# An exact integer addition of a weight conversion goes from VectorE to GpSimd, with another hand-written order of the opening

## The chip, the cores and the metric

One core of a Trainium2 chip runs the whole program. The metric is the device time of one execution in microseconds (us). "PE" is TensorE, "DVE" VectorE, "ACT" ScalarE, "POOL" GpSimd, and "SP" the engine whose queue issues most DMAs.

## The reference

Eight batches of an attention with two sparse masks (a local one for the first four heads, a strided one for the other four), then a feed-forward block on the 4608 tokens. The weights come as 64-bit floats.

```
scores = scale * np.matmul(q, k.transpose(0, 1, 3, 2))      # 8 x 8 heads, 576 x 576, D = 64
mask_local = (rel >= 0) & (rel < 32)
mask_strided = (rel >= 0) & (pos[None, :] % 32 == pos[:, None] % 32)
attn = softmax(where(mask, scores, -1e9));  x = attn @ v      # (4608, 512)
h = np.maximum(np.maximum(x @ w1, x @ w2), x @ w3)            # 512 -> 768
out = h @ w_out                                               # 768 -> 512
```

## The kernel before

Tokens are worked in nine chunks of 512. Attention goes in 32 units of two heads: units 0 to 3 are batch 0, 4 to 7 batch 1, and within a batch the first two are strided, the last two local. Every float32 matrix product is made of three float32r products (high times high, high times low part, low times high).

Each of the 24 weight tiles (128 x 512 values; 0 to 17 for w1, w2, w3, then 18 to 23 for w_out) lands as 64-bit words, and the kernel builds the float32 value out of the bits before it splits it into a high and a low part. Up to the end of the first chunk (chunk 0) all engines follow one order written out by hand, the string `OPENING`, in steps of a letter and a number. Each engine takes its own instructions in just this order. The letters:

- A: ACT takes the magnitude of the high words (L144) and scales the low words (L145); POOL clamps the magnitude (L146). The result lies in a `work` tile, of which there are three in turn.
- B: three DVE instructions. L158 shifts the bits into a scratch that lies in the upper halves of two banks of the PSUM tile `o_ps`; L161 joins them with the sign bits; L164 adds the rounding as an integer. The trace shows L164 as a custom DVE operation on 1024 elements of 16 bits.
- C: ACT copies the high part (L172), POOL subtracts to get the low part (L173). The `work` tile is free after that.
- S, X, E, N: scores on PE, less maximum on DVE, exponential on ACT, sums, probabilities and a transpose on DVE, for one unit. V: values on PE into `o_ps`. H and L: ACT (L417) and DVE (L421) copy `o_ps` out as high and low parts; `o_ps` is a single tile, so the next V waits for L.
- F: 12 matmuls of the first product for chunk 0 (L436) into one of two `f_ps` tiles; F of number n uses weight tile n. M: the maximum, by ACT (L447) or DVE (L449), and after every third the split by ACT (L452) and POOL (L453). O and Q: second product (18 matmuls, L462), copy and store. U: a rearranging copy on ACT.

In matmuls of PE, S of a unit below 8 has 132 in a strided unit (4 that write the mask, L257, and 128, L288) and 76 (4 and 72) in a local one; V has 128 (L400) in a strided unit of batches 0 and 1 and 84 (L359) in a local one. All loads stand in SP's queue in one order: the operands of units 0 to 3 with weight tiles between them, then weights and units 4 and 5; the loads of later units are issued at S and V. After the opening, chunks 1 to 8 run in a loop that the diff doesn't touch.

Before, PE's part of the order up to its first F is S0 S1 S2 V0 S3 V1 V2 S4 V3 F0.

Of the kernel before, what the change touches and what calls it, by code (L numbers as in the profile page):

```python
# [9 lines left out]
I32 = mybir.dt.int32  # L10
U32 = mybir.dt.uint32
AF = mybir.ActivationFunctionType
ALU = mybir.AluOpType
AX = mybir.AxisListType

B, H, S, D = 8, 8, 576, 64
# [28 lines left out]


OPENING = """
A0 S0 X0 E0 N0 S1 X1 B0 E1 S2 A1 N1 C0 X2 V0 A2 B1 B2 H0 C1 S3 A3 L0 X3 V1 E2 E3 N2 C2 H1 L1 V2 N3 A4 S4
H2 A5 L2 B3 C3 X4 E4 B4 C4 V3 H3 N4 L3 F0 A6 B5 A7 F1 C5 B6 M0 C6 M1 A8 S5 B7 X5 C7 A9 B8 E5 F2 F3 C8 M2
N5 V4 A10 A11 M3 F4 B9 C9 B10 F5 C10 H4 M4 A12 S6 M5 X6 A13 F6 B11 B12 F7 M6 C11 L4 F8 C12 B13 E6 M7 A14  # L50
C13 V5 A15 A16 F9 M8 B14 C14 B15 A17 B16 M9 C15 B17 A18 C16 A19 F10 M10 F11 C17 B18 F12 C18 M11 H5 M12
N6 F13 A20 F14 L5 A21 B19 V6 C19 A22 M13 F15 B20 C20 M14 F16 M15 A23 F17 B21 M16 B22 C21 C22 S7 M17 B23
X7 C23 H6 O0 E7 L6 N7 U8 O1 Q0 O2 V7 S8 Q1 H7 L7 O3 Q2 Q3
"""


# [1 line left out]
def fused_kernel(ctx, tc, qT, kT, qk_loc, qk_str, v_loc, v_str, m_loc, m_str, w1, w2, w3, w_out, out):  # L58
    nc = tc.nc
# [20 lines left out]
    pin = tc.keep_in_program_order  # L80
# [17 lines left out]
    for sign in (1, -1):  # L98
        pin(nc.gpsimd.affine_select(
            out=unit, in_=unit, pattern=[[-sign, P]], base=0, channel_multiplier=sign, compare_op=ALU.is_ge, fill=0.0  # L100
# [21 lines left out]
    raws, begun, weight = [], [], {}  # L122
# [14 lines left out]
    def convert_begin():  # L137


        raw, i, j = raws.pop(0)  # L140
        words = raw.rearrange("p (n two) -> p n two", two=2)
        low, high = words[:, :, 0], words[:, :, 1]
        mag = wk.tile([P, 512], F32, name="work")
        pin(nc.scalar.activation(out=mag, in_=high.bitcast(F32), func=AF.Abs))  # L144
        pin(nc.scalar.activation(out=low, in_=low.bitcast(U32), func=AF.Copy, scale=2.0**-29))  # L145
        pin(nc.gpsimd.tensor_scalar(out=mag, in0=mag, scalar1=W_MOST, scalar2=W_LEAST, op0=ALU.min, op1=ALU.max))  # L146
        begun.append((low, high, mag, i, j))

    converted = []

    def convert_bits():

        low, high, mag, i, j = begun.pop(0)
        banks = len(weight) + len(converted)
        psum = o[:, banks % 2 * 2 : banks % 2 * 2 + 2, 256:].bitcast(I32)
        bits = mag.bitcast(I32)
        halves = lambda x: x.rearrange("p (a f) -> p a f", a=2)
        pin(nc.vector.tensor_scalar(  # L158
            out=psum, in0=halves(bits), scalar1=3, scalar2=0x3FFFFFF8, op0=ALU.logical_shift_left, op1=ALU.bitwise_and
        ))  # L160
        pin(nc.vector.scalar_tensor_tensor(  # L161
            out=halves(bits), in0=halves(high), scalar=-0x40000000, in1=psum, op0=ALU.bitwise_and, op1=ALU.bitwise_or
        ))
        pin(nc.vector.tensor_tensor(out=bits, in0=bits, in1=low, op=ALU.add))  # L164
        converted.append((mag, i, j))

    def convert_end():

        mag, i, j = converted.pop(0)
        parts = wt.tile([P, 2, 512], F32R, name=f"w{i}_{j}")  # L170
        hi, lo = parts[:, 0, :], parts[:, 1, :]
        pin(nc.scalar.copy(out=hi, in_=mag))  # L172
        pin(nc.gpsimd.tensor_tensor(out=lo, in0=mag, in1=hi.bitcast(F32), op=ALU.subtract))  # L173
        weight[i, j] = [x if i is None else x.rearrange("p (c f) -> p c f", c=NKC) for x in (hi, lo)]
# [251 lines left out]
    def ff_in(c, j, i):  # L426
        if not ps_f:
            early_ps.close()
            ps_f.append(ctx.enter_context(tc.tile_pool(name="ps_f", bufs=2, space=bass.MemoryType.PSUM)))
        f_ps = ps_f[0].tile([P, 512], F32, name="f_ps")  # L430
        hi, lo = x_chunk(c)
        wh, wl = weight[i, j]

        for kc in (2, 3, 0, 1):
            for n, (w, x) in enumerate(((wh, hi), (wh, lo), (wl, hi))):
                pin(nc.tensor.matmul(  # L436
                    f_ps, w[:, kc, :], x[:, kc, :], start=(kc == 2 and n == 0), stop=(kc == 1 and n == 2)
                ))
        hs[c, j, i] = f_ps

    def ff_max(c, j, i):
        f_ps = hs.pop((c, j, i))
        if i == 0:
            hs[c, j] = hm.tile([P, CH], F32, name="h_max")
        a = hs[c, j]
        if i == 0:
            pin(nc.scalar.copy(out=a, in_=f_ps))  # L447
        else:
            pin(nc.vector.tensor_tensor(out=a, in0=f_ps, in1=a, op=ALU.max))  # L449
        if i == 2:  # L450
            hh, hl = hs[c, j] = hp.tile([P, CH], F32R, name="hh"), hp.tile([P, CH], F32R, name="hl")
            pin(nc.scalar.copy(out=hh, in_=a))  # L452
            pin(nc.gpsimd.tensor_tensor(out=hl, in0=a, in1=hh.bitcast(F32), op=ALU.subtract))  # L453
# [24 lines left out]
    for n in (2, 3):  # L478
# [9 lines left out]
    steps = {  # L488
        "U": paired_queries, "S": scores, "X": less_maximum, "E": exponentials, "N": lambda n: (probabilities(n), transposed(n)),
        "V": values, "H": leading, "L": rest,  # L490
        "A": lambda n: convert_begin(), "B": lambda n: convert_bits(), "C": lambda n: convert_end(),
        "F": lambda n: ff_in(0, n // 3, n % 3), "M": lambda n: ff_max(0, n // 3, n % 3),
        "O": lambda n: ff_out(0, n), "Q": lambda n: ff_store(0, n),
    }
    for step in OPENING.split():
        what, n = step[0], int(step[1:])
# [8 lines left out]
    for c in range(1, NCHUNK):  # L505
# [4 lines left out]
        for i in range(3 * NJ + CH // P):  # L510
            if i in BURSTS and c < B - 1:
                n = 4 * (c + 1) + BURSTS.index(i)
# [98 lines left out]
```

## Time and profile before

| | |
|---|---|
| median of 3 runs | 716.47 us (713.24 to 718.65) |
| the profiled execution | 712.11 us |
| its span, first to last instruction | 710.4 us |
| PE busy | 680.8 us (96%) |
| DVE, ACT, POOL busy | 311.7, 185.3, 122.6 us |
| first F matmul | 46.44 us after the start |

The profiled execution has its own time. The page gives busy time by engine; the windows give it by stretch; the timeline shows each engine's instructions in order, with the idle time before them in brackets and what ended it. "issue" there is a wait that no semaphore in the profile explains.

### The profile page before, as it was taken

To read this page: it belongs to the slowest core of one execution; us is meant where nothing else is said; L and a number is where in the kernel's file an instruction comes from. 1 tells how busy PE (TensorE), PEld (TensorE's weight loads), DVE (VectorE), ACT (ScalarE), POOL (GpSimd) and SP (SyncE) were. 2 spreads that over 40 slices of the span, in tenths; PEclk is the share of its full clock that TensorE was granted. 3 is DMA by queue.
4 is the path that set the end of the run, shared out by engine and by line. 5 is a ranking of instruction groups with operands and counts; after the bars stand their busy time and mean duration, and the time that the engine had idled before them with its cause. 6 is when DMAs were issued, how large, how long until landed. Compare 5 with 4: busy or idle time off the path is not lost.

```text
span 710.4 us, 17277 instructions
## 1 busy us (share of the span) xinstructions
PE 680.8 (96%) x7680; PEld 559.6 (79%) x7680; DVE 311.7 (44%) x527; ACT 185.3 (26%) x394; POOL 122.6 (17%) x129
## 2 busy tenths in 40 slices
PE   5469899999999999999999999999999999999997
PEld 4358677888888888888888888888888888888886
DVE  5778996455504551444344443544155201101110
ACT  1546563312222222213122222222222111111111
POOL 4336573001101110111001100110001101100110
PEclk9869999999999999999999999999999999999999
DMA  8998101222311222112321231223120010010001
GB/s 238 269 303 305 52 31 64 96 72 73 102 48 55 64 85 94 55 56 65 109 70 54 65 102 51 81 66 93 42 64 2 16 45 1 0 43 17 1 1 59
DMA packets 35803, 55.26 MB, mean 78 GB/s; under 512 B 5200, under 2 KB 18512, under 8 KB 35728
## 3 DMA queue, kind: packets, MB, share of 16 engines
q1 hardware_dynamic: 30016, 44.19, 21.3%
q10 hardware_dynamic: 5712, 9.96, 3.8%
q8 instruction: 60, 0.98, 0.6%
q14 instruction: 15, 0.12, 0.1%
HBM read 44.70 MB, written 9.44 MB: 76 GB/s over the span
## 4 chain that ended last, share of the span: by engine, by line
PE 88%; DVE 4%; DMA 2%; issue 2%; POOL 1%; ACT 1%; SPq 1%; DVEq 0%; POOLq 0%; ACTq 0%
PE f_ps L436 59%; PE f_ps L462 20%; PE o_ps L359 2%; PE s_ps L288 2%; PE o_ps L389 2%; PE s_ps L266 2%; DMA w<-in_w 2%; DVE work L164 1%; DVE work L161 1%; DVE o_ps L158 1%; SPq L228 1%; POOL wNone L173 1%; PE o_ps L400 0%; DMA v_t<-in_v_loc 0%; DVE xl L421 0%
## 5 line engine op out<-in xcount | busy, mean ns | idle before, releaser
L436 PE MATMUL f_ps<-xh,w 128*128 128x512 f32 x1296 | 409.2, 392 | 2.8 <-ACT h_max L447 1.8
L436 PEld LDWEIGHTS f_ps<-xh,w 128*128 128x128 f32 x1296 | 243.9, 188 | 56.5 <-ACT h_max L447 2.3
L436 PE MATMUL f_ps<-xl,w 128*128 128x512 f32 x648 | 252.9, 390 | 0.0
L449 DVE TENSOR_TENSOR h_max<-f_ps,h_max 128x512 f32<-128x512 f32 x108 | 74.4, 689 | 286.1 <-PE f_ps L436 285.9
L453 POOL TENSOR_TENSOR hl<-h_max,hh 128x512 fp32r<-128x512 f32 x54 | 69.4, 1286 | 516.5 <-ACT hh L452 516.5
L436 PEld LDWEIGHTS f_ps<-xl,w 128*128 128x128 f32 x648 | 122.0, 188 | 24.5
L462 PE MATMUL f_ps<-wNone,hh 128*128 128x512 f32 x432 | 134.2, 392 | 0.2 <-POOL wNone L173 0.2
L462 PEld LDWEIGHTS f_ps<-wNone,hh 128*128 128x128 f32 x432 | 80.5, 188 | 17.4 <-POOL wNone L173 0.7
L452 ACT CAST hh<-h_max 128x512 fp32r<-128x512 f32 x54 | 33.4, 619 | 197.8 <-DVE h_max L449 197.8
L462 PE MATMUL f_ps<-wNone,hl 128*128 128x512 f32 x216 | 84.1, 389 | 0.0
L421 DVE TENSOR_TENSOR xl<-o_ps,xh 128x320 fp32r<-128x320 f32 (+11 forms) x96 | 28.3, 350 | 55.5 <-ACT xh L417 44.7
L447 ACT COPY h_max<-f_ps 128x512 f32<-128x512 f32 x54 | 31.7, 587 | 62.8 <-POOL hl L453 32.0
L467 ACT COPY work<-f_ps 128x512 f32<-128x512 f32 x36 | 21.2, 588 | 101.5 <-PE f_ps L462 101.5
L462 PEld LDWEIGHTS f_ps<-wNone,hl 128*128 128x128 f32 x216 | 40.5, 188 | 8.5
L316 ACT ACTIVATE s_ps<-s_ps 128x640 f32<-128x640 f32 (+2 forms) x32 | 20.2, 633 | 88.3 <-DVE s_ps L312 87.8
L417 ACT CAST xh<-o_ps 128x320 fp32r<-128x320 f32 (+11 forms) x96 | 24.3, 328 | 32.2 <-PE o_ps L389 18.8
L333 DVE STREAM_TRANSPOSE pt<-s_ps 128x640 f32<-128x640 f32 (+2 forms) x32 | 31.3, 979 | 0.7
L288 PE MATMUL s_ps<-qk_t 64*32 64x64 f32 (+1 forms) x1664 | 22.6, 227 | 7.1 <-issue 5.1
L311 DVE TENSOR_REDUCE mx<-s_ps 128x10 f32<-128x640 f32 (+2 forms) x32 | 24.1, 752 | 10.0 <-PE s_ps L288 9.2
L288 PEld LDWEIGHTS s_ps<-qk_t 64*32 64x32 f32 x1664 | 19.3, 117 | 11.4 <-issue 8.6
L173 POOL TENSOR_TENSOR w<-work,w 128x512 fp32r<-128x512 f32 x18 | 23.4, 1301 | 25.6 <-ACT w L172 25.6
L359 PEld LDWEIGHTS o_ps<-pt,v_t 32*64 32x64 f32 x1344 | 17.6, 141 | 10.6 <-issue 6.2
(52 smaller groups left out, 362.3 us busy)
## 6 DMA issues: line engine op xcount, KB each, us to landing
out<-work ACTq DMA_DIRECT2D x36, 256.0 KB
w<-in_w SPq DMA_DIRECT2D x17, 512.0 KB
qk_t<-in_qT SPq DMA_DIRECT2D x28, 288.0 KB
qk_t<-in_kT SPq DMA_DIRECT2D x28, 288.0 KB
v_t<-in_v_str SPq DMA_DIRECT2D x48, 128.0 KB
v_t<-in_v_loc SPq DMA_DIRECT2D x48, 96.0 KB
wNone<-in_w_out SPq DMA_DIRECT2D x6, 512.0 KB
v_t<-in_v_str SPq DMA_DIRECT2D x16, 72.0 KB
```

The source lines that it names most:

```text
L173: pin(nc.gpsimd.tensor_tensor(out=lo, in0=mag, in1=hi.bitcast(F32), op=ALU.subtract))
L288: pin(nc.tensor.matmul(s_ps[32 * j : 32 * (j + 1), h, k1 : k1 + w], t[hs, q0 : q0 + 32], t[hs, k0 : k0 + w], start=not first, stop=not fir ...
L333: pin(nc.vector.transpose(pt[:, :, : nm * at], s_ps[:, :, : nm * at]))
L359: pin(nc.tensor.matmul(o[h * D : (h + 1) * D, j, 32 * max(m, 0) : 32 * max(m, 0) + width], v[js, h, m + 1, :], pt[js, h, m * TK + 32 : m * ...
L417: pin(nc.scalar.copy(out=hi, in_=src))
L421: pin(nc.vector.tensor_tensor(out=lo, in0=src, in1=hi.bitcast(F32), op=ALU.subtract))
L436: pin(nc.tensor.matmul(f_ps, w[:, kc, :], x[:, kc, :], start=(kc == 2 and n == 0), stop=(kc == 1 and n == 2)))
L447: pin(nc.scalar.copy(out=a, in_=f_ps))
L449: pin(nc.vector.tensor_tensor(out=a, in0=f_ps, in1=a, op=ALU.max))
L452: pin(nc.scalar.copy(out=hh, in_=a))
L453: pin(nc.gpsimd.tensor_tensor(out=hl, in0=a, in1=hh.bitcast(F32), op=ALU.subtract))
L462: pin(nc.tensor.matmul(f_ps, h[:, ts], w, start=(j == 0 and n == 0), stop=(j == NJ - 1 and n == 2)))
```

## The change

The third instruction of B, the integer addition, becomes a step of its own, D, as a plain integer `tensor_tensor` on GpSimd. C follows D. The scratch's place alternates as before. The order of the opening is another one; on PE it now goes S0 S1 V0 S2 S3 V1 V2 S4 V3 F0, and S7 stands ahead of V6. The order of the loads ahead of the opening is the same.

```diff
--- before.py
+++ after.py
@@ -45,12 +45,13 @@
 
 
 OPENING = """
-A0 S0 X0 E0 N0 S1 X1 B0 E1 S2 A1 N1 C0 X2 V0 A2 B1 B2 H0 C1 S3 A3 L0 X3 V1 E2 E3 N2 C2 H1 L1 V2 N3 A4 S4
-H2 A5 L2 B3 C3 X4 E4 B4 C4 V3 H3 N4 L3 F0 A6 B5 A7 F1 C5 B6 M0 C6 M1 A8 S5 B7 X5 C7 A9 B8 E5 F2 F3 C8 M2
-N5 V4 A10 A11 M3 F4 B9 C9 B10 F5 C10 H4 M4 A12 S6 M5 X6 A13 F6 B11 B12 F7 M6 C11 L4 F8 C12 B13 E6 M7 A14
-C13 V5 A15 A16 F9 M8 B14 C14 B15 A17 B16 M9 C15 B17 A18 C16 A19 F10 M10 F11 C17 B18 F12 C18 M11 H5 M12
-N6 F13 A20 F14 L5 A21 B19 V6 C19 A22 M13 F15 B20 C20 M14 F16 M15 A23 F17 B21 M16 B22 C21 C22 S7 M17 B23
-X7 C23 H6 O0 E7 L6 N7 U8 O1 Q0 O2 V7 S8 Q1 H7 L7 O3 Q2 Q3
+A0 S0 X0 B0 E0 D0 C0 S1 N0 X1 E1 N1 V0 S2 H0 L0 A1 A2 B1 X2 E2 S3 D1 B2 V1 D2 A3 C1 C2 H1 N2 X3 A4 B3 D3
+B4 L1 E3 D4 A5 C3 N3 V2 C4 H2 B5 S4 A6 B6 L2 D5 X4 D6 V3 C5 A7 C6 H3 L3 A8 A9 F0 B7 D7 B8 M0 D8 C7 F1 B9
+D9 F2 A10 C8 M1 E4 C9 M2 B10 F3 A11 N4 A12 D10 M3 F4 B11 M4 D11 B12 S5 F5 V4 C10 C11 D12 A13 M5 C12 X5
+B13 F6 A14 M6 F7 D13 E5 A15 B14 M7 F8 B15 D14 N5 C13 D15 A16 F9 C14 C15 H4 M8 A17 F10 M9 A18 S6 B16 F11
+M10 D16 B17 D17 C16 X6 C17 B18 A19 E6 D18 M11 L4 B19 A20 F12 F13 V5 C18 N6 D19 M12 B20 M13 A21 F14 D20
+B21 C19 H5 D21 C20 F15 A22 C21 A23 M14 L5 B22 D22 B23 D23 M15 C22 F16 M16 S7 C23 F17 X7 E7 M17 V6 O0 O1
+H6 L6 N7 U8 Q0 V7 S8 H7 O2 Q1 O3 Q2 Q3 L7
 """
 
 
@@ -151,7 +152,7 @@
     def convert_bits():
 
         low, high, mag, i, j = begun.pop(0)
-        banks = len(weight) + len(converted)
+        banks = len(weight) + len(converted) + len(added)
         psum = o[:, banks % 2 * 2 : banks % 2 * 2 + 2, 256:].bitcast(I32)
         bits = mag.bitcast(I32)
         halves = lambda x: x.rearrange("p (a f) -> p a f", a=2)
@@ -161,7 +162,14 @@
         pin(nc.vector.scalar_tensor_tensor(
             out=halves(bits), in0=halves(high), scalar=-0x40000000, in1=psum, op0=ALU.bitwise_and, op1=ALU.bitwise_or
         ))
-        pin(nc.vector.tensor_tensor(out=bits, in0=bits, in1=low, op=ALU.add))
+        added.append((low, mag, i, j))
+
+    added = []
+
+    def convert_add():
+        low, mag, i, j = added.pop(0)
+        bits = mag.bitcast(I32)
+        pin(nc.gpsimd.tensor_tensor(out=bits, in0=bits, in1=low, op=ALU.add))
         converted.append((mag, i, j))
 
     def convert_end():
@@ -488,7 +496,8 @@
     steps = {
         "U": paired_queries, "S": scores, "X": less_maximum, "E": exponentials, "N": lambda n: (probabilities(n), transposed(n)),
         "V": values, "H": leading, "L": rest,
-        "A": lambda n: convert_begin(), "B": lambda n: convert_bits(), "C": lambda n: convert_end(),
+        "A": lambda n: convert_begin(), "B": lambda n: convert_bits(), "D": lambda n: convert_add(),
+        "C": lambda n: convert_end(),
         "F": lambda n: ff_in(0, n // 3, n % 3), "M": lambda n: ff_max(0, n // 3, n % 3),
         "O": lambda n: ff_out(0, n), "Q": lambda n: ff_store(0, n),
     }
```

## Rows read from the trace of the kernel before

**Rows 1.** The page: busy time by engine, and the granted clock in 40 slices.
```profile
PE 680.8 (96%) x7680; PEld 559.6 (79%) x7680; DVE 311.7 (44%) x527; ACT 185.3 (26%) x394; POOL 122.6 (17%) x129
PEclk9869999999999999999999999999999999999999
```

**Rows 2.** Windows: length; busy us of PE, PEld, DVE, ACT, POOL; clock, DMA share, GB/s.
```profile
0.00:46.44 46.44, 23.94 (x972) 19.13 (x972) 30.98 (x58) 15.96 (x31) 16.00 (x38) 0.81 0.96 271
46.44:116.00 69.56, 66.28 (x862) 52.42 (x858) 64.00 (x98) 42.76 (x82) 44.95 (x44) 0.98 0.43 134
116.00:710.40 594.40, 590.59 (x5852) 488.01 (x5852) 216.68 (x372) 126.59 (x283) 61.64 (x48) 1.00 0.18 56
```

**Rows 3.** Timeline of PE, 12 to 47 us: start, us, what, [idle before].
```profile
12.39 0.67 PE L288 MATMUL s_ps<-qk_t 64*32 64x18 f32 x42 [2.21 <-issue]
12.98 2.50 PE L257 MATMUL s_ps<-mloc,unit 128*128 128x320 f32 x4
15.41 1.36 PE L288 MATMUL s_ps<-qk_t 64*32 64x64 f32 x72
...
19.98 1.92 PE L400 MATMUL o_ps<-pt,v_t 18*64 18x18 f32 x120 [2.86 <-issue]
...
24.26 1.24 PE L288 MATMUL s_ps<-qk_t 64*32 64x64 f32 x72
27.89 0.79 PE L400 MATMUL o_ps<-pt,v_t 18*64 18x18 f32 x59 [2.38 <-DVE xl L421]
30.80 1.26 PE L400 MATMUL o_ps<-pt,v_t 18*64 18x18 f32 x69 [2.13 <-issue]
33.72 1.26 PE L359 MATMUL o_ps<-pt,v_t 32*64 32x64 f32 x59 [1.66 <-DVE xl L421]
36.10 0.67 PE L359 MATMUL o_ps<-pt,v_t 32*64 32x64 f32 x25 [1.12 <-issue]
...
41.97 0.44 PE L288 MATMUL s_ps<-qk_t 64*32 64x18 f32 x30 [2.85 <-issue]
44.86 1.66 PE L359 MATMUL o_ps<-pt,v_t 32*64 32x64 f32 x84 [2.44 <-DVE work L161]
46.44 0.80 PE L436 MATMUL f_ps<-xh,w 128*128 128x512 f32 x1
```

**Rows 4.** DMA queues, 17 to 18 and 39 to 40 us: packets, MB, share.
```profile
q8 instruction: 1, 0.02, 9.5%
...
q8 instruction: 1, 0.02, 7.2%
```

**Rows 5.** Timeline of PE after F0: its two longest idle times.
```profile
87.62 0.50 PE L436 MATMUL f_ps<-xh,w 128*128 128x512 f32 x1 [1.85 <-ACT h_max L447]
...
91.41 0.50 PE L436 MATMUL f_ps<-xh,w 128*128 128x512 f32 x1 [0.77 <-DVE h_max L449]
```

**Rows 6.** Groups by line and shape, 0 to 150 us: busy us, mean ns.
```profile
L173 POOL TENSOR_TENSOR w<-work,w 128x512 fp32r<-128x512 f32 x18 | 23.4, 1301 | 25.6 <-ACT w L172 25.6
...
L158 DVE TENSOR_SCALAR o_ps<-work 128x512 int32<-128x512 int32 x24 | 16.5, 687 | 3.4 <-PE o_ps L400 2.2 <-POOL work L146 0.5 <-PE o_ps L359 0.3
L146 POOL TENSOR_SCALAR work<-work 128x512 f32<-128x512 f32 x24 | 15.7, 659 | 22.1 <-ACT work L144 22.0
L164 DVE CUSTOM_DVE_ANT_0 work<-w,work 128x1024 uint16<-128x1024 uint16 x18 | 15.6, 869 | 1.7
...
L161 DVE SCALAR_TENSOR_TENSOR work<-w,o_ps 128x512 int32<-128x512 int32 x18 | 12.4, 687 | 0.7
...
L453 POOL TENSOR_TENSOR hl<-h_max,hh 128x512 fp32r<-128x512 f32 x7 | 9.1, 1299 | 25.9 <-ACT hh L452 25.9
...
L164 DVE CUSTOM_DVE_ANT_0 work<-wNone,work 128x1024 uint16<-128x1024 uint16 x6 | 6.5, 1084 | 0.6
```

**Rows 7.** Lines L164 and L173: durations, shortest, median, longest ns.
```profile
L164 DVE CUSTOM_DVE_ANT_0 work<-wNone,work x6: 693/782/1805, 92.9 to 112.0; 128x1024 uint16<-128x1024 uint16 x6
...
L173 POOL TENSOR_TENSOR w<-work,w x18: 1265/1290/1523, 21.3 to 94.7; 128x512 fp32r<-128x512 f32 x18
```

## The prediction

> **What bounds the kernel now.** I read the page first: PE is busy for 96% of the span, and the granted clock is full from the fourth slice on [rows 1]. Then three windows, cut at the first F (46.44 us) and at the end of O0 (116 us) [rows 2]. After 116 us PE is idle for 3.8 us in 594: nothing that this change touches can shorten that. Between 46.44 and 116 PE is idle for 3.28 us of 69.56, with DVE busy for 64.0 and POOL for 44.95. Ahead of 46.44 it is idle for 22.5 us. So all that can be won or lost lies in two sums, 22.5 us ahead of F0 and 3.3 us behind it; PE's work itself doesn't change.
>
> Ahead of F0 the timeline of PE shows what the idle time waits for [rows 3]. Five of the waits, 2.21, 2.86, 2.13, 1.12 and 2.85 us, 11.2 in all, are called "issue" and fall in the middle of a step, where no semaphore is waited for. Counting matmuls by the steps' sizes (132, 132, 76, 128, 76, 128, 84, 132 for S0 S1 S2 V0 S3 V1 V2 S4), the rows restart at matmul 222 (42 of S1 are left), 348 (120 of V0 left), 603 (69 of V1), 731 (25 of V2) and 858 (30 of S4). The distances are multiples of about 127; the one place that is missing, about 476, lies in S3. With its weight load a matmul is two instructions, so this is a grid of some 254 instructions. The DMA view shows packets of an instruction queue, one of 0.02 MB, in 17 to 18 us and in 39 to 40 us, shortly ahead of the restarts at 19.98 and 41.97 [rows 4]. So PE waits there for its own program, which comes by DMA while the DMA engines are 0.96 busy [rows 2]. The times fit a window of two blocks, the next being asked for when one is used up: matmul 476 was passed at about 24.3 and 603 restarted at 30.80, 6.5 us later; 603 was reached at 28.68 and 731 came at 36.10, 7.4 later; 731 was reached at 34.98 and 858 came at 41.97, 7.0 later [rows 3].
>
> The Trainium skill ("Runtime: NRT & Kernel Launch", section "Instruction fetch mechanics") has just this window of two 16 KiB blocks of 256 instructions, but says that crossing a block is mostly hidden. By that rule the 11.2 us would have another cause, and the new order could not lose by them; this is the first rival below. The trace disagrees while the loads fill the DMA engines.
>
> **The change part by part.** *DVE loses the addition*: 18 at 869 ns and 6 at 1084 ns [rows 6], 15.6 + 6.5 = 22.1 us. Some 19 of them lie behind F0, where DVE was 92% busy and where PE's two long waits, 1.85 and 0.77 us, are for the emptying of `f_ps` by ACT and DVE [rows 5], held up in the queues of conversions. With DVE down from 64.0 to about 45 us of 69.6 these waits go; I keep 0.4 of the 3.28 us of idle time. What is late next there is POOL.
>
> *POOL gains 24 integer additions.* None is in the trace. The nearest row is its subtraction L173, also two inputs of 512 values, at 1301 ns [rows 6], hardly ever longer than 1290 (longest 1523) [rows 7]. The lower end is the clamp with one input, 659 ns [rows 6]. The upper end is two subtractions, 2.6 us, if POOL had to go by halves of 16 bits as the record of the DVE operation does (1024 elements [rows 6]). I take 1.29, the row with the same number of inputs: 24 x 1.29 = 31 us more, beside PE's matmuls. Behind F0 POOL then has 17 tiles (seven are converted ahead of F0 in the new order) of 0.66 + 1.29 + 1.29 and six h splits of 1.30 [rows 6], 55.1 + 7.8 = 62.9 us. PE has 66.3 us of work up to the end of O0 [rows 2], whose last group, 0.7 us, is the first to need POOL's last results. So POOL fits, with 2.7 us to spare. It is nearly full, and I expect PE to wait little for it: only the w_out tiles come just in time, since tiles 7 to 17 are needed at 2.8 us each plus attention and POOL delivers one in 3.7 us with a lead of seven.
>
> The Trainium skill ("GPSIMD Engine Reference", section "Key points") speaks against the move: elementwise work is about twice as fast on VectorE. By that rule, at 1.29 for 0.69 us and with every addition on the path, the change would cost 24 x 0.6 = 14 us. The rows agree on the durations: the shortest L164 took 693 ns. But beside POOL's work it took up to 1805 ns, while POOL's subtraction hardly stretched [rows 7], and the addition lies beside matmuls; so I take nothing of the 14 us.
>
> *The order ahead of F0.* V0 now goes ahead of S2. V0 can start when S1 ends (about 13.05), runs 84 matmuls to number 348 and stands until 19.98 as before, since that block was asked for when S1 passed 222, which hasn't moved. Before, this wait was filled by S2, 2.50 + 1.36 us, with only 8 of V0 [rows 3]; now only V0's 84, 1.3 us, stand ahead of it and S2 comes after. Matmul 476 is passed at 19.98 + 0.7 (44 of V0) + 3.8 (S2) + 2.5 (the mask matmuls of S3) = 27.0 instead of 24.3. The next block follows 6.5 us later, at 33.5 (30.80 before); V1 ends at 34.8.
>
> Then B3 and B4 now stand ahead of L1 on DVE; before they came behind V2. They write their scratch into `o_ps`, so they wait for V1 and H1, as L158 is seen to wait for L400 [rows 6]; V2 waits for L1. From V1's end to V2 it was 1.66 us [rows 3]; with two B of 0.687 + 0.687 [rows 6] it is 4.4: V2 starts at 39.3 and reaches 731 at 40.5 (34.98 before). The block behind comes 7.0 later, 47.5; S4's last 30 matmuls 0.44, V3 1.66, and F0 starts at 49.6. Before, V3 waited another 2.44 us for the L161 of a B [rows 3]; now S4 is later than DVE and that wait is gone. So F0 is 49.6 - 46.44 = 3.1 us later: two block waits carry +5.5, less 2.44.
>
> *What moves at no cost*: D0, C0 and the early conversions lie on POOL and ACT, which were busy for 16 of 46 us ahead of F0 [rows 2]; if POOL were late there, C6 would still not be needed before F6. S7 ahead of V6 changes the order of two loads in SP's queue, for units of the next chunk. O2 behind V7 and S8 is work that PE has in either order. At F0 PE starts at the same reduced clock as before, after the same idle time [rows 1].
>
> *The sum*: +3.1 ahead of F0, -2.9 behind it: +0.2 us on the profiled execution's 712.11, 712.3. That execution was 4.4 us below the median of the runs, 716.47; against the median I forecast 716.7.
>
> **The rivals.**
> 1. *The blocks don't hold PE* (the fetch is not tied to the position in the program, or the later requests find shorter queues). For it: the one at about 476 cost nothing. Against it: five restarts on the grid. If only the first came as early as before, F0 would be at 32.06 + 1.66 + 2.75 + 1.26 + 7.0 + 0.44 + 1.66 = 46.8, +0.4 and -2.5 in all; with neither, V2 ends at 38.2, S4 takes 2.8 (its own time before, without the wait) and V3 1.66, so 42.7, -3.7 and -6.6 in all. DVE's B5, B6 and L2 stand ahead of V3 and keep it from the lower end: I take -4.5, 712.0.
> 2. *POOL becomes the bound, slower.* It decides from the point where 17 additions use up the 2.7 us to spare, 1.29 + 0.16 = 1.45 us each. At 1.9 us it is 17 x 0.45 = 7.7 us behind F0, less the waits already gone: +0.2 + 7.7 = about 724; at 2.6 us 19.6, 736. For it: the stride of 8 bytes in the low words and an integer type that no POOL row shows. Against: the flat 1.29 of two-input rows.
> 3. *The blocks take longer.* The one asked for at 222 (10.18) came at 19.98, 9.8 us later [rows 3]. With that for both, F0 is 3.3 + 2.8 = 6.1 us later still: 722.8.
> 4. *The addition is lowered to something else than one POOL instruction*: then POOL's row isn't there and DVE keeps its 22 us; the order alone would give 3.1 us and up to the old 3.3 behind F0, +3.1 or about 719.6.
>
> **How the numbers follow.** Forecast 0.52, rival 1 0.2, rival 2 0.12, rival 3 0.13, rival 4 0.03. About 1%, 7.2 us, is what a measurement of this kernel can tell from no change: the three runs lie 5.4 us apart. Faster by more needs more than rival 1's lower end: 0.06 with the scatter. Slower by more: rival 2 from 1.9 us, and the upper end of rival 3 with the scatter, 0.13. The rest, 0.81, is within. The range goes from 711 (rival 1, with a us of scatter) to 724 (rivals 2 at 1.9 us and 3); left out are rival 2's dearer prices.
>
> **What the profile after would show.** The addition as a POOL row of 24 near 1.29 us; DVE near 289.6 us, POOL near 153.6. PE's "issue" waits at matmuls 222, 348, 603 and 858 again; no restart before 19.98 in V0, with some 5 us of idle time there; F0 near 49.6; behind F0 less than 1 us of idle time on PE. Wrong would be: an F0 ahead of 46.5 (the count of blocks or the wait of B3 for H1 is wrong), a POOL addition over 1.45 us, or PE waiting for POOL in O0.

## The result

The changed kernel takes 707.33 us (706.89 to 707.39, four runs) against 715.92 us (713.24 to 718.65, four runs) of the kernel before: the ratio is 0.9879, with an interval of 0.984 to 0.9917. It is faster by 1.2%, and its time lies below the predicted range. The profiled execution took 707.39 us, that of before 712.11.

The page of the changed kernel: busy time by engine, the granted clock in 40 slices, and the shares of the chain that ended last.

```profile
PE 680.0 (96%) x7680; PEld 560.5 (79%) x7680; DVE 290.5 (41%) x503; ACT 185.6 (26%) x394; POOL 151.3 (21%) x153
PEclk9769999999999999999999999999999999999999
PE 94%; DVE 2%; DMA 1%; issue 1%; SPq 1%; ACT 0%; POOL 0%; POOLq 0%; DVEq 0%
```

DVE has 21.2 us less than in [rows 1], POOL 28.7 more, PE the same work. Windows of the changed kernel, cut at its first F and at 116 us, with the columns of [rows 2]:

```profile
0.00:42.00 42.00, 21.73 (x973) 17.87 (x973) 29.21 (x54) 19.23 (x36) 27.54 (x48) 0.81 0.90 269
42.00:116.00 74.00, 72.43 (x914) 58.45 (x909) 47.65 (x83) 41.48 (x81) 61.98 (x58) 0.95 0.45 147
116.00:705.70 589.70, 585.89 (x5827) 484.18 (x5808) 213.64 (x366) 124.91 (x277) 61.77 (x48) 1.00 0.18 56
```

F0 starts at 42.00 instead of 46.44 us. Behind it PE is idle for 1.57 of 74.00 us instead of 3.28 of 69.56, with DVE at 64% of that stretch (92% before) and POOL at 84% (65% before). The timeline of PE in the changed kernel shows both; its lines answer to [rows 3] (S is L265 and L296 now, V L408 and L367, F L444):

```profile
10.99 0.66 PE L296 MATMUL s_ps<-qk_t 64*32 64x18 f32 x42 [0.90 <-issue]
13.05 1.47 PE L408 MATMUL o_ps<-pt,v_t 18*64 18x18 f32 x85 [1.39 <-DVE pt L341]
15.28 0.88 PE L408 MATMUL o_ps<-pt,v_t 18*64 18x18 f32 x43 [0.77 <-issue]
16.09 2.50 PE L265 MATMUL s_ps<-mloc,unit 128*128 128x320 f32 x4
...
25.30 1.75 PE L408 MATMUL o_ps<-pt,v_t 18*64 18x18 f32 x128 [3.44 <-DVE work L162]
33.40 1.65 PE L367 MATMUL o_ps<-pt,v_t 32*64 32x64 f32 x84 [6.35 <-DVE xl L429]
36.36 1.32 PE L265 MATMUL s_ps<-mstr,unit 128*128 128x144 f32 x4 [1.31 <-DVE pt L341]
...
40.05 0.44 PE L296 MATMUL s_ps<-qk_t 64*32 64x18 f32 x29 [1.26 <-issue]
40.42 1.65 PE L367 MATMUL o_ps<-pt,v_t 32*64 32x64 f32 x84
42.00 0.80 PE L444 MATMUL f_ps<-xh,w 128*128 128x512 f32 x1
...
64.93 0.82 PE L408 MATMUL o_ps<-pt,v_t 18*64 18x18 f32 x63 [1.57 <-issue]
```

The waits named "issue" still fall at the same counts, 222 (42 of S1 left), 349 (43 of V0 left), 859 (29 of S4 left) and, behind F0, 1241 (63 of V4 left). But ahead of F0 they are 0.90, 0.77 and 1.26 us, 2.9 in all where before had 11.2, and V3's wait of 2.44 us is gone. Behind F0 there is one wait only, in V4; no F waits for ACT or DVE as in [rows 5]. A wait named "issue" at such a count is called a block wait below. The addition itself, by line and shape, and then shortest, median and longest:

```profile
L172 POOL TENSOR_TENSOR work<-work,w 128x512 int32<-128x512 int32 x18 | 23.4, 1300 | 5.3 <-DVE work L162 3.6 <-POOL work L172 0.8 <-POOL w L181 0.4
L172 POOL TENSOR_TENSOR work<-work,wNone 128x512 int32<-128x512 int32 x6 | 7.8, 1311 | 0.5 <-DVE work L162 0.5
L172 POOL TENSOR_TENSOR work<-work,w x18: 1278/1300/1327, 11.1 to 83.5; 128x512 int32<-128x512 int32 x18
```

It is one POOL instruction of 1.30 us, as long as the subtraction [rows 7] and flatter.

One quantity orders all that follows: the start of chunk 1, which is the first L436 or L444 behind O3 on PE's timeline. In ten profiled executions of the two kernels the time is that start plus 581.1 to 581.2 us, so the whole difference lies ahead of it: 131.04 us before, 126.18 after. Each run below is told by its median time and the ratio to the kernel before in the same session, then by F0 and the stretch from F0 to chunk 1 in its profiled execution.

### The profile page after: what moved, and what is told of

Read it like the earlier page. It is cut to its first block, busy times and chain, and to the rows that moved or that the text cites. A ratio compares the mean times of both kernels' runs of the same rounds, so it can differ in the third digit from the quotient of the medians.

```text
span 705.7 us, 17268 instructions
## 1 busy us (share of the span) xinstructions
PE 680.0 (96%) x7680; PEld 560.5 (79%) x7680; DVE 290.5 (41%) x503; ACT 185.6 (26%) x394; POOL 151.3 (21%) x153
## 4 chain that ended last, share of the span: by engine, by line
PE 94%; DVE 2%; DMA 1%; issue 1%; SPq 1%; ACT 0%; POOL 0%; POOLq 0%; DVEq 0%
PE f_ps L444 64%; PE f_ps L470 21%; PE o_ps L367 2%; PE s_ps L296 2%; PE o_ps L397 2%; PE s_ps L274 2%; DMA w<-in_w 1%; SPq L236 1%; PE s_ps L265 1%; PE o_ps L408 0%; DVE o_ps L159 0%; DVE work L162 0%; DVE pt L341 0%; DVE s_ps L334 0%; SPq L206 0%
## 5 line engine op out<-in xcount | busy, mean ns | idle before, releaser
L444 PE MATMUL f_ps<-xh,w 128*128 128x512 f32 x1296 | 410.2, 394 | 0.0
L444 PEld LDWEIGHTS f_ps<-xh,w 128*128 128x128 f32 x1296 | 244.9, 189 | 52.8
L444 PE MATMUL f_ps<-xl,w 128*128 128x512 f32 x648 | 253.8, 392 | 0.0
L444 PEld LDWEIGHTS f_ps<-xl,w 128*128 128x128 f32 x648 | 122.7, 189 | 24.8
L475 ACT COPY work<-f_ps 128x512 f32<-128x512 f32 x36 | 21.2, 590 | 104.3 <-PE f_ps L470 104.3
L367 PEld LDWEIGHTS o_ps<-pt,v_t 32*64 32x64 f32 x1344 | 17.5, 141 | 11.4 <-DVE xl L429 6.5
L296 PE MATMUL s_ps<-qk_t 64*32 64x64 f32 (+1 forms) x1664 | 21.9, 222 | 4.2 <-issue 2.2
L367 PE MATMUL o_ps<-pt,v_t 32*64 32x64 f32 (+1 forms) x1344 | 19.3, 236 | 6.3 <-DVE xl L429 6.3
L296 PEld LDWEIGHTS s_ps<-qk_t 64*32 64x32 f32 x1664 | 18.7, 114 | 8.1 <-issue 6.6
```

The costliest lines, as they stand in the source:

```text
L296: pin(nc.tensor.matmul(s_ps[32 * j : 32 * (j + 1), h, k1 : k1 + w], t[hs, q0 : q0 + 32], t[hs, k0 : k0 + w], start=not first, stop=not fir ...
L367: pin(nc.tensor.matmul(o[h * D : (h + 1) * D, j, 32 * max(m, 0) : 32 * max(m, 0) + width], v[js, h, m + 1, :], pt[js, h, m * TK + 32 : m * ...
L444: pin(nc.tensor.matmul(f_ps, w[:, kc, :], x[:, kc, :], start=(kc == 2 and n == 0), stop=(kc == 1 and n == 2)))
```

## The experiments

**Both kernels again** ("old order" is that of before, "new order" that of the change).

> The kernel before, profiled again. Theory A (PE's waits for its own program vary with the state of the DMA queues): the five issue waits ahead of F0 sum to something else than 11.2 us, F0 moves with them (44 to 50 us) and the device time moves by the same amount; the runs of this kernel spread by some 5 us. Theory B (the waits belong to the order): the five waits come again within 0.5 us each and F0 at 46.4.

Measured: 715.27 us, 1.001 (0.9995 to 1.0026); F0 46.85 and 85.2 us behind it, in a profiled execution of 713.25. The block waits ahead of F0 are 2.44, 1.77, 1.64 and 4.32, 10.2 in all: single waits changed by up to 2.1 us (V1 has none now), as theory A says, but F0 hardly moved.

> The changed kernel, profiled again. Theory A: issue waits ahead of F0 other than 2.9 us in sum, F0 between 40 and 46 us. Theory B: 2.9 us again, F0 at 42.0. Either way the ratio stays near 0.988.

Measured: 707.74 us, 0.9901 (0.9882 to 0.9919); F0 43.07, then 82.7. The block waits ahead of F0 are 0.8 us in all, S1's alone (theory A again); V4's is again 1.56.

**One part at a time.** The order alone: the changed kernel with

```diff
-        pin(nc.gpsimd.tensor_tensor(out=bits, in0=bits, in1=low, op=ALU.add))
+        pin(nc.vector.tensor_tensor(out=bits, in0=bits, in1=low, op=ALU.add))
```

> The new order, but step D adds on DVE. If the order alone makes the gain (theory O): ratio near 0.988 to 0.992, F0 near 42 to 44 us. If the engine makes it (theory E, relief of DVE): F0 3 us later than with the addition on POOL and idle time of PE behind F0 of 3 us or more, ratio 0.996 to 1.005.

Measured: 714.02 us, 0.9982 (0.9967 to 0.9997). F0 is early, at 43.41, but 87.15 us follow. PE's timeline of this kernel:

```profile
55.85 0.50 PE L444 MATMUL f_ps<-xh,w 128*128 128x512 f32 x1 [1.61 <-DVE h_max L457]
80.08 0.50 PE L444 MATMUL f_ps<-xh,w 128*128 128x512 f32 x1 [1.10 <-DVE h_max L457]
91.58 0.50 PE L444 MATMUL f_ps<-xh,w 128*128 128x512 f32 x1 [0.84 <-DVE h_max L457]
```

With two shorter ones of 0.39 and 0.38 these are 4.3 us in which F waits for the maximum on DVE, behind additions that take 945 ns in the mean (the 18 of w1 to w3). No block wait shows in V4 here. What the order wins ahead of F0, DVE takes back.

The move alone: the old order, with the line `nc.vector.tensor_tensor` of the addition changed to `nc.gpsimd.tensor_tensor` in its place directly behind B.

> The old order, with the addition on POOL directly behind B. Theory O: F0 stays near 46.4 us, and at most the 3.3 us of idle time behind F0 go, or grow since POOL is in the way of the conversions; ratio 0.996 to 1.005. Theory E: ratio near 0.99.

Measured: 724.41 us, 1.0131 (1.0113 to 1.0149); F0 46.22, then 97.2. The window from F0 to 124 us, the groups of lines by shape in it, and PE's longest wait:

```profile
46.22:124.00 77.78, 68.08 (x860) 53.89 (x855) 45.37 (x74) 41.07 (x76) 65.91 (x62) 0.94 0.38 119
```

```profile
L164 POOL TENSOR_TENSOR work<-work,w 128x512 int32<-128x512 int32 x13 | 16.9, 1307 | 1.2 <-DVE work L161 1.2
...
L172 ACT CAST w<-work 128x512 fp32r<-128x512 f32 x14 | 8.7, 619 | 20.6 <-POOL work L164 20.6
```

```profile
92.45 0.79 PE L436 MATMUL f_ps<-xh,w 128*128 128x512 f32 x1 [5.23 <-ACT h_max L447]
```

POOL is busy for 85% of the stretch, and the addition has its 1.30 us. But ACT, whose C step stands in its queue ahead of the maximum of the next F, waits 20.6 us for additions, and PE behind it: up to chunk 1 its waits for ACT are 9.0 us, for POOL 0.85, and a block wait in S5 is 1.91. This order has five C ahead of F0; the new one has seven, and it also puts other steps between a D and its C. Neither theory has this, and the parts don't add up: -0.9 us for the order and +9.5 for the move (both against 714.94), -7.2 for the two together.

**Early or late ahead of F0.** S2 back in front of V0, in the changed kernel: `N1 V0 S2 H0` becomes `N1 S2 V0 H0`.

> The changed kernel with S2 ahead of V0 on PE, as before the change. By the prediction's step (V0 ahead of S2 lets the wait for the block at 349 go unfilled) V1 ends 2.7 us earlier than in the changed kernel and F0 comes earlier by up to 2.7 us. By the rival (V1 waits for the B2 of a weight tile that lands at 21 to 24 us, whatever PE does ahead of it) V1 starts at 25 to 27 us all the same and F0 stays at 42 to 43 us.

Measured: 707.22 us, 0.9902 (0.9876 to 0.9928). F0 45.97, then 80.6. Neither reading came: F0 is later than in the changed kernel. V1 starts at 27.29, and block waits of 1.18, 1.73, 1.65, 3.52 and 0.90 us are back ahead of F0, 9.0 in all, but V4 has none. The granted clock is given as 1.00 over the whole span, yet the first matmuls of F0 take as long as those of the other kernels at 0.50 (0.63 us for one of `xl`, 0.39 further on), so that row can't be taken at its word here:

```profile
46.56 0.63 PE L444 MATMUL f_ps<-xl,w 128*128 128x512 f32 x1
...
52.35 0.39 PE L444 MATMUL f_ps<-xl,w 128*128 128x512 f32 x1
```

The same kernel profiled once more, for the spread of its waits:

> The changed kernel with S2 ahead of V0, once more. By the build: the block for 349 starts 6.2 us after count 222, F0 at 46 us. By the execution: if the block comes within 3 us, F0 is at 42 to 43 us, which would say that the order of S2 and V0 is worth nothing by itself.

Measured: 710.30 us, one execution; F0 44.01, then 85.1; V4 waits 1.43 here. So with S2 ahead F0 came at 45.97 and 44.01, behind the 42.0 to 43.4 of the changed kernel's four profiles.

L1 ahead of B3 and B4 on DVE, in the changed kernel: `H1 N2 X3 A4 B3 D3 B4 L1 E3 D4` becomes `H1 N2 L1 X3 A4 B3 D3 B4 E3 D4`.

> The changed kernel with L1 ahead of X3, B3 and B4 on DVE. If the chain V1, H1, B3, B4, L1, V2 over the PSUM tile holds PE (V2 waits 6.35 us in the changed kernel), V2 starts 3 to 4 us earlier, and F0 by 1 to 2 us, since the next block of the program and N3 then come last; time down by 1 to 2 us. If V2's early start is worth nothing, F0 stays at 42 to 43 us.

Measured: 709.06 us, 0.9915 (0.989 to 0.9941); F0 45.65, then 82.8: later and not earlier. V1 has a block wait of 3.03 here, and V2 waits nearly as long as in the changed kernel, for another step of DVE, as PE's timeline shows:

```profile
36.67 1.65 PE L367 MATMUL o_ps<-pt,v_t 32*64 32x64 f32 x84 [6.11 <-DVE work L162]
```

L162 is the second instruction of B4. V2 needs the scratch in `o_ps` to be read as well as L1's copy, so the two B stand ahead of V2 wherever L1 is.

The grid itself: 64 or 128 small matmuls more ahead of the opening, into a place of `o_ps` that nothing reads (work added, nothing left out). Each turn of the loop is two matmuls in the trace.

```diff
+    for k in range(32):        # 64 in the second
+        half, j = slice(k % 2 * D, (k % 2 + 1) * D), 32 * (k // 2 % 4)
+        pin(nc.tensor.matmul(o[j : j + 32, 2 + k % 2, 480:498], unit[half, :32], unit[half, :18], start=True, stop=True))
     for step in OPENING.split():
```

> The changed kernel with 64 small matmuls more at the start of PE's program, in its first 2.8 us, which are idle. If the issue waits sit on a grid of the program's own instructions, the restarts come again at the same count from the start (222, 349, 859, 1241), that is 64 matmuls earlier in the steps: in S1 with 106 left, in V0 with 107 left, in S4 with 93 left, ahead of V4. If they belong to the steps, S1 restarts with 42 left and V4 with 63. Time within 1 us of the changed kernel's.

Measured: 712.16 us, 0.9962 (0.994 to 0.9983); F0 46.83, then 82.2. That is 4.4 us over the 707.74 of the changed kernel's second measurement, where at most 1 was expected. The restarts move by 64 matmuls in the steps and stay on the grid in the count: 106 of S1 left instead of 42, 107 of V0 instead of 43; V1 now waits 4.35 us with 4 left, and V3 has a wait, 3.24 us with 50 left.

> As the shift by 64, but by 128 small matmuls, one whole period of the grid, so that the restarts fall back to the places in the steps that they have in the changed kernel. If the 4.4 us that the shift by 64 cost come from where in the steps the blocks of the program end, they go: within 1.5 us of the changed kernel, no issue wait in V3. If the extra matmuls themselves cost the time, it costs as much again: 4 us or more over the changed kernel.

Measured: 709.09 us, 0.9902 (0.9883 to 0.9921); F0 47.21, then 80.7. That is 1.35 us over 707.74, within the 1.5 of the first reading. The restarts are back at 42 of S1, 43 of V0 and 29 of S4; V3 and V4 have none. PE's timeline of the second, three of its five block waits:

```profile
14.44 0.66 PE L296 MATMUL s_ps<-qk_t 64*32 64x18 f32 x42 [2.91 <-issue]
19.54 0.88 PE L408 MATMUL o_ps<-pt,v_t 18*64 18x18 f32 x43 [3.05 <-issue]
...
32.01 1.26 PE L408 MATMUL o_ps<-pt,v_t 18*64 18x18 f32 x68 [3.96 <-issue]
```

So PE does wait for its program by the count. And this run has 13.2 us of block waits ahead of F0, and a later F0 than the 46.44 of before, and is still 1% faster: what it gains lies behind F0, in a stretch without V4's wait.

Loads held back: in the changed kernel the loads from weight tile 8 and unit 5 on are issued only after a small SP transfer that reads `xl` of L1.

```diff
-    load_weights(6)
-    load_qk(5)
-    load_v(5)
-    load_weights(len(sources))
...
+        if step == "L1":
+            pin(nc.sync.dma_start(out=gate, in_=xl[0][:, 3, 0:1].bitcast(F32)))
+            load_weights(6)
+            load_qk(5)
+            load_v(5)
+            load_weights(len(sources))
```

> The changed kernel with the loads from weight tile 8 on (with those of unit 5) held back until L1 by a small transfer ahead of them in SP's queue, which waits for L1. If the blocks of the program are late because they stand behind these loads, the block for 859 is served within 2 us of the count 731 and S4 doesn't wait for it; F0 up to 1 us earlier. If they are late for another reason, S4 waits as before. In either case tile 8 lands some 3 us later, ahead of its use at about 43 us.

Measured: 706.81 us, 0.987 (0.9847 to 0.9892); F0 42.58, then 83.3. S4 doesn't wait, V0's wait is longer (2.11), F0 stays: V3 now waits 0.98 us for a copy on DVE. The time can't be told from that of the changed kernel. Nor does S4 wait in the changed kernel's second profile, without any holding back, so this run doesn't show that these loads make the blocks late.

V3 without the B4 ahead of it, in the kernel before: `X4 E4 B4 C4 V3 H3 N4 L3 F0` becomes `X4 E4 V3 H3 L3 B4 C4 N4 F0`.

> The kernel before with B4 and C4 (and N4) behind V3, H3 and L3 instead of ahead. The prediction's term: V3 no longer waits 2.44 us for the L161 of B4. If that term is right, F0 comes 2.3 us earlier, at 44.1 to 44.5 us, and the time falls by about 2 us (ratio 0.997), less if the conversions, now later, let PE wait more behind F0. If another step takes its place, F0 stays at 46.4.

Measured: 717.34 us, 1.0022 (1.0006 to 1.0038). V3's wait is gone and F0 is at 44.99, but 91.9 us follow, with a block wait of 3.81 us in S5 at 57.73. The time didn't fall. (Two later profiles of the unchanged kernel have F0 at 44.60 and 45.04 too, with V3's wait, so this F0 can't be put down to the edit.)

**V4 later**: in the changed kernel `S5 F5 V4 C10 ... X5 B13 F6` becomes `S5 F5 C10 ... X5 F6 V4 B13`, so that the 12 long matmuls of F6 lie between S5 and V4.

> The changed kernel with V4 (and B13) behind F6 instead of ahead of it, so that 12 long matmuls more lie between S5 and V4. If PE waits for a block of its program in V4 (1.57 us in both profiles of the changed kernel), the wait is gone and the time falls by about 1.5 us (ratio to the kernel before 0.988 where the changed kernel has 0.990). If the wait is something of V4 itself, it moves along and the time stays.

Measured: 704.22 us, 0.9855 (0.9829 to 0.9882): the fastest version here. It lies 3.1 us below the changed kernel's 707.33 by the medians, and 1.7 to 3.3 us by the ratios of the two kernels in their sessions, so the size is less sure than the sign. V4's wait is gone and no other comes. F0 is at 42.14. Windows from F0 to chunk 1 in three executions: this kernel, the changed kernel, and the kernel before in the execution of 715.23 us that is told below.

```profile
42.14:122.52 80.38, 80.38 (x1065) 65.58 (x1061) 50.70 (x90) 43.25 (x87) 62.11 (x59) 0.98 0.49 161
```

```profile
42.00:126.18 84.18, 82.61 (x1066) 67.08 (x1061) 50.80 (x90) 43.38 (x87) 61.98 (x58) 0.95 0.46 149
```

```profile
44.60:134.03 89.43, 83.72 (x1066) 66.47 (x1061) 69.89 (x110) 46.84 (x92) 45.09 (x44) 0.98 0.41 132
```

The same matmuls are busy for 80.38, 82.61 and 83.72 us, since more of them run at the lower of the two clock levels (1.2 instead of 2.4 GHz, 0.50 in the windows). In the second and third these are some behind the block wait: from 60 to 70 us the granted clock is 1.00 in this kernel and 0.85 in the changed one. In all three the first matmuls of F0 are slow too; the clock is given as 0.50 there in the first two, but as 1.00 in the third, where they take just as long. So moving V4 shortened the stretch by 3.8 us, 1.57 of waiting and 2.23 of PE's busy time. Two other kernels of the new order without a wait behind F0, S2 first and the shift by 128, have the same 80.6 and 80.7 us; those with V4's wait have 82.7 to 85.1.

**How far one execution speaks for the kernel.** The profiled execution of before lay 4.4 us under the median that I had. So single executions of both kernels were profiled again.

> The changed kernel once more, for the time that a block of the program takes from the count at which it is asked for to its packet. If that belongs to the build, the block for 349 starts 2.3 to 2.7 us after count 222, as in its two profiles, and F0 comes at 42 to 43.1 us. If it belongs to the execution, it can be 5 to 7 us, and F0 45 to 46 us.

Measured: 708.26 us; F0 43.37, then 83.7. V0 restarts at 17.40, two us later than in the first profile, yet V1 starts at 25.71:

```profile
17.40 0.88 PE L408 MATMUL o_ps<-pt,v_t 18*64 18x18 f32 x43 [2.77 <-issue]
25.71 1.44 PE L408 MATMUL o_ps<-pt,v_t 18*64 18x18 f32 x128 [1.29 <-DVE work L162]
```

By the DMA view the block's packet starts 3.6 us after count 222 was reached, so not in the 2.3 to 2.7 of the first reading, though F0 isn't late. V1 waits for B2, and the trace gives B2 its start by the clamp of weight tile 2, for whose landing ACT waits. ACT's timeline of the first profile:

```profile
22.44 0.66 ACT L145 ACTIVATE work<-w 128x512 f32<-128x512 f32 x1 [3.46 <-DMA w<-in_w]
```

That wait ends at 22.44, 23.87, 22.84 and 22.88 in the four profiles of the changed kernel, and V1 starts 2.86 or 2.87 us later in each, whether V0 waited or not. What V0 loses comes out of a wait that stands anyway.

> The same once more: by the build 2.3 to 2.7 us and F0 at 42 to 43.1 us, by the execution anything from 2 to 7 us.

Measured: 708.81 us; F0 42.57, then 85.0; V0 restarts at 17.15, the packet 3.8 us after count 222, as by the execution; V1 starts at 25.74.

> The kernel before once more: by the build the block for 348 starts 5.8 to 6.9 us after count 222, as in its two profiles; by the execution it can be 2.5 us. F0 at 46.2 to 46.9 us in either case, since S4's last block and the wait for B4 come last.

Measured: 712.94 us; F0 46.33, then 85.4; no block wait behind F0; the packet 6.1 us after count 222, as by the build (but 4.3, 5.2 and 4.7 in the three below). So three profiles of before lay between 712 and 713.3 with medians of 714 to 716. Three more were taken.

> The kernel before, unchanged. Three profiled executions of it took 712.1, 713.3 and 712.9 us, while its medians were 714 to 716; the changed kernel's four lay at 707.0 to 708.8 and its medians at 707.3 to 707.7. So 2 to 4 us of the difference of the medians have no profile. If the longer executions of before are longer by PE's block waits ahead of F0, an execution of 715 us or more shows an issue sum some 2 to 4 us over 11.2 and an F0 later than 47.5, with the 85 us from F0 to the first matmul of chunk 1 as before. If they are longer behind F0, F0 stays at 46.3 to 46.9 and that stretch is 87 us or more. An execution of 712 to 713 tells nothing of it.

Measured: 717.64 us; F0 45.04, then 91.4.

> The same kernel once more, the same two readings: longer by the block waits means F0 later than 47.5 at an unchanged 85 us behind it; longer behind F0 means F0 near 46.5 and 87 us or more; 712 to 713 tells nothing.

Measured: 720.39 us; F0 49.89, then 89.3; block waits of 2.52, 0.96, 0.69, 0.54 and 4.63 us ahead of F0.

> The same kernel a third time, the same two readings: longer by the block waits means F0 later than 47.5 at an unchanged 85 us behind it; longer behind F0 means F0 near 46.5 and 87 us or more; 712 to 713 tells nothing.

Measured: 715.23 us; F0 44.60, then 89.4. All three are longer behind F0, the second reading; only the execution of 720.39 is late at F0 as well. All three have a block wait behind F0 that the shorter executions don't have, 2.82, 2.44 and 2.38 us with 15 matmuls of S5 left. PE's timeline of the last one:

```profile
17.82 1.92 PE L400 MATMUL o_ps<-pt,v_t 18*64 18x18 f32 x120 [0.68 <-issue]
...
44.60 0.80 PE L436 MATMUL f_ps<-xh,w 128*128 128x512 f32 x1
...
52.88 1.13 PE L288 MATMUL s_ps<-qk_t 64*32 64x18 f32 x113
56.40 0.34 PE L288 MATMUL s_ps<-qk_t 64*32 64x18 f32 x15 [2.38 <-issue]
```

The place is matmul 1113 (972 ahead of F0, 24 of F0 and F1, 117 of S5), 127 behind 986. By the timeline 986 was passed some 13 matmuls into F0 and F1, at 49.8, and 1113 was reached at 54.0; the block came 6.6 us after the first. In the execution of 712.11 us the same two places are 50.8 and 55.0, the same 4.2 us apart, and there the block was there in time. The DMA view shows the packet itself: for this block it starts at 53.8 here and at 52.3 there, 4.0 and 1.5 us behind 986, and in the execution of 712.94 at 49.9, 1.4 us ahead of 986. At every block wait of the ten profiles of the two kernels PE goes on 2.4 to 3.4 us after the packet's start; what differs is when the packet starts. With that wait, the two on `f_ps` (1.87 and 0.76) and some shorter ones PE is idle for 5.71 us from F0 to chunk 1 here, and the clock is 0.83 in the window from 50 to 60 us.

## Why the prediction was wrong

**The addition on POOL** was right: 1.30 us (1.29 taken), DVE 290.5 us (289.6), POOL 151.3 (153.6) and 62.0 of them from F0 to 116 us (62.9), and PE waits for POOL nowhere behind F0. (The subtraction's 1290 ns is its median in [rows 7], not a length that it hardly ever exceeds; nothing hangs on it.) Rival 2's mechanism exists all the same, at the price of 1.30 and not from 1.45 up: the move alone in the old order made ACT wait for POOL and cost 9.5 us. So the order decides the sign of the move. The new order's two more tiles ahead of F0, and the steps that it puts between a D and its C, are the likely reasons; no run takes them apart. I had counted that lead as time to spare, but not asked what the move is worth without it.

**The step that failed first** is "V0 ... stands until 19.98 as before, since that block was asked for when S1 passed 222, which hasn't moved". It took the time that a block needs as a constant. In four profiles of the changed kernel V0 restarts at 15.28, without a wait, at 17.40 and at 17.15; six profiles of before have it at 17.82 to 19.98. All that was built on it falls: V1 has no block wait, S4's is 1.26 us and ends at 40.05 instead of 47.5, and F0 came 4.4 us earlier instead of 3.1 later. V1's end, put at 34.8 us, was 27.05.

What the runs showed in its place: in the changed kernel's profiles the path up to V1 goes through weight tile 2 and not through the blocks. In the old order L0 stands behind B2 on DVE, and V1 starts 4.5 to 4.9 us after tile 2's landing in all six profiles; in the new one L0 is done ahead of B1, and it is 2.9. By the means of six and four profiles V1 starts 1.7 us earlier for it, and from V1's start to F0 another 2.1 us go, V3's wait of 2.44 among them: 3.8 us ahead of F0 in all. That wait was rightly forecast to go. V2's start was rightly tied to B3, B4 and L1, but the term was too small: 6.35 us from V1's end to V2 (6.35 to 7.74 in the four) instead of 4.4, since N2 and X3 hold DVE ahead of B3. (And 34.8 plus 4.4 is 39.2, not 39.3.)

F0 came where rival 1 "with neither" wait had put it, 42.7 us, with 42.0 to 43.4 in four profiles, but by luck: it had V2 end at 38.2 and S4 run without a wait in 2.8, where V2 ended at 35.05 and 5.4 us passed from there to V3. I gave the rival a chance of 0.2 and, for DVE's sake, a price of only -4.5.

**The term behind F0** had the right cause: the two waits on `f_ps` went with DVE's load, and the order alone, with the addition still on DVE, kept 4.3 us of them. Two things were missing. The changed kernel has a block wait of its own in V4, 1.57 us (1.56 to 1.85 in three other profiles), and the clock is 0.85 in the window from 60 to 70 us around it; moving V4 took both away, 3.8 us of the stretch. So of 3.28 us of idle time 1.7 went here and not 2.9. The second thing is the block wait in S5 that half the profiles of before have and that the prediction's one execution didn't show.

**The step to the median failed too**: "That execution was 4.4 us below the median ...; against the median I forecast 716.7" carries the gap over as if it belonged to the measurement. By the profiles it belongs to the old order. Three of six profiled executions of before wait in S5 for the block of 1113, and these are the ones of 715.2 us and more; the two other kernels of that order that were profiled, the move alone and V3 first, wait there too. Only F0 and F1 stand between 986 and S5 there, 4.2 us of work up to 1113. In the new order F0 to F4 stand there: in the changed kernel's profile 986 is passed at about 47.1 and 1113 at 59.2, 12 us later, and S5 waits in none of its four profiles. The times of these four lie within 2 us (707.0 to 708.8), those of the six of before within 8 (712.1 to 720.4).

**The sum, by executions near both medians** (715.23 and 707.39 us): F0 from 44.60 to 42.00 is -2.6 us; the stretch behind it from 89.43 to 84.18 is -5.25, of which 5.71 - 1.57 = 4.14 are PE's idle time and 1.11 PE's busy time. That is -7.85, and the times differ by 7.84. Against the faster execution of 712.11 it is -4.4 and -0.4. By the means of all six profiles of before and four of the changed kernel it is -3.8 ahead of F0 and -3.7 behind it, -7.4 in the time. So the gain has two sources of about one size; the one behind F0 is -1.2 us against the three profiles of before without S5's wait and -6.1 against the three with it.

By the Trainium skill ("Runtime: NRT & Kernel Launch", section "Instruction fetch mechanics") crossing a block is mostly hidden. The runs agree where the matmuls of a block are long, as from F0 to F4 (12 us between two blocks, no wait), and disagree where S and V go through 127 of them in 4.2 us while loads fill the DMA engines (waits of 1.56 to 1.85 us in V4 of the changed kernel, 2.38 to 2.82 in S5 of before).

**What stays open**: why the packet of a block starts when it does. It differs between executions of one kernel. For the block of V0 it starts 2.2 to 3.8 us after count 222 was reached in the four profiles of the changed kernel and 4.3 to 6.8 us in the six of before. Yet V3 first, which is the kernel before up to there, has 2.8, and S2 first, the changed kernel up to V0, has 6.1: this doesn't show that the order of the steps decides it. Why the old order's first blocks ahead of F0 are slower in some executions, and faster in two of the three that wait in S5, no run tells. Nor is the size of the clock's share apart from the wait's settled by an experiment of its own.

## What to carry to other kernels

Before moving work to another engine, ask who waits for it there, and how far ahead its new owner can run: here the same 1.30 us on POOL cost 9.5 us in the old order, with five tiles done ahead, and gained 6.3 us in the new one, with seven, over the order alone. When PE's idle time follows the count of instructions, look at the time between two places on that grid, and lay long matmuls between them where it is shorter than the fetch took in the profiles; V4 behind F6 is such a move, and its profile is 3.8 us shorter than the changed kernel's. And where executions of one kernel spread by 1%, profile several before a forecast rests on one: the gap between a profile and a median can be a wait that the change removes.

## What the runs showed that I had not expected

The time of an instruction block is not a property of the program: for one and the same place, matmul 1113 of the kernel before, the packet started 1.4 us ahead of matmul 986 in the execution of 712.94 us and 4.0 us behind it in that of 715.23. So a block can be asked for before PE has passed the count at which the prediction has it asked for: the count gives the place of a wait, but not the moment of the request.

And an earlier F0 isn't an earlier end by itself: the changed kernel with S2 ahead of V0 starts F0 4.0 us later and ends within 0.3 us of the changed kernel's profile, since it has no wait in V4 and its stretch behind F0 is 3.6 us shorter.
